# Twelve of the second layer's sixteen output chunks by seven products of combinations, in four sweeps of four chunks

## The chip, the cores and the metric

One Trainium2 chip, one core of it. The metric is the device time of one execution in microseconds (us), a median over runs. Engines are named as in the profile: PE is TensorE (PEld its weight loads), DVE is VectorE, ACT is ScalarE, POOL is GpSimd, SP issues the DMAs.

## The reference, cut to what matters

```python
x = attention(q, k, v)            # 2304 tokens x 512, sliding window
h = x @ moe_w_in                  # 512 -> 2048
x = elu(h) @ moe_w_out            # 2048 -> 512
h = x @ moe2_w_in                 # second layer, same shapes
g = h * (1.0 / (1.0 + np.exp(-h)))
return g @ moe2_w_out             # 2304 x 512
```

Here it is about the last line: g (2304 tokens x 2048) times moe2_w_out (2048 x 512).

## The kernel before, in words

The tokens are three blocks of 768 (`BIG`), each cut into two halves of 384 (`HALF`); the hidden width of 2048 is sixteen chunks of 128. Both layers run in sweeps over chunks: `SWEEPS` (line 174) gives the second layer the chunks 0 to 6, 6 to 12 and 12 to 16. A **step** is one sweep of one block; `steps` (lines 195, 196) lists them, six of the first layer (a first sweep of four chunks was done beside the attention) and nine of the second, in the order of `ORDER` (line 182). The block that ends one sweep begins the next.

Every operand is split into a high and a low fp32r part (`split_weight`, lines 328 to 335, for weights: ACT copies the high part, DVE subtracts). A product is three matmuls: high by high, high by low, low by high.

In a step the hidden values of two chunks at a time (a **quad**, lines 1031 to 1102) are made by seven products of combinations in place of eight: six matmuls of 384 columns each (line 1051). The seven input combinations are the tiles `c`, made on DVE and ACT for a block's first sweep (`make`, lines 920 to 951; for the second layer's first step ahead of time, `make_far`), stored, and loaded again for each later sweep of another block (`reload`, lines 985 to 988, 7 x 768 KB): each is loaded as soon as the last quad of the step before has read that tile. Of the seven accumulated results, ACT copies out three (`snap`, line 1060) and DVE adds to three (line 1064); `activated` (lines 1005 to 1029) then writes, for each of a quad's four results (two chunks x two halves), SiLU by ACT twice (lines 1014, 1015: plain, and rounded to the high part) and the low part by one DVE subtraction (line 1029).

Then `outputs` (lines 1104 to 1163) multiplies by w_out. In the second layer a group is one tile of 128 tokens: for each chunk of the sweep three matmuls of 512 columns (line 1143), all into one PSUM bank; afterwards the bank is copied to (first sweep, ACT, line 1155) or added to (DVE, line 1157) the block's accumulator `acc`. In the last sweep each finished tile is stored (line 1161). The first half's three groups follow the quads; the second half's three are owed to the next step and are merged into its first nine products (`merge`, `SPAN`, lines 1169 to 1205).

Weights come through four raw buffers (`weight`, lines 337 to 394): 64-bit input, turned into fp32 by one POOL, one ACT and two DVE operations (lines 358 to 363) for each of the 32 chunks of a layer, then split. Chunks of w_in go in pairs into three buffers of combinations (`form`, line 387), chunks of w_out into a ring of seven (`OUTS`).

All this is not issued in program order: `Plan` (lines 35 to 133) is a list scheduler that the kernel runs while it is built. Each operation has an engine, a cost in us, the keys it reads and writes, and a due time; per engine the ready operation that is latest is issued next. The chip then runs each engine's list in that fixed order.

Of the kernel before, what the change touches and what calls it, by code (L numbers as in the profile page):

```python
# [22 lines left out]
def f32(ap):  # L23
    return ap.bitcast(F32)
# [112 lines left out]
def attention_elu_silu_kernel(  # L137
# [33 lines left out]
        for g in range(g0, g0 + n):  # L171
            home[g] = bi, (g - g0) * P

    SWEEPS = [(0, 4), (4, 10), (10, 16)], [(0, 6), (6, 12), (12, 16)]
    FIRST_F = SWEEPS[0][0][1]
    MOST_F = 6
    NRAW = 4
# [1 line left out]
    BIG = 6 * P  # L179
    HALF = BIG // 2  # L180
    NBIG = NT // BIG
    ORDER = ((0, 1, 2), (2, 1, 0)), ((2, 1, 0), (0, 1, 2), (2, 1, 0))
    PAIRS, OUTS, BANKS = 3, 7, 3
    GS = 6, 7
    SPAN = 9
# [7 lines left out]
    BURST = 99  # L193

    steps = [(0, sw + 1, b) for sw in range(2) for b in ORDER[0][sw]]
    steps += [(1, sw, b) for sw in range(3) for b in ORDER[1][sw]]
    FAR = 6

    plan = Plan()
# [4 lines left out]
    def matmuls(n, w):  # L204
        return n * (w + 32) / 2400.0
# [85 lines left out]
    bank_n = [0]  # L291
    banks = [BANKS]

    def bank():
        i = bank_n[0] % banks[0]
        bank_n[0] += 1
        return ("m", i)
# [7 lines left out]
                for f in range(f0, f1):  # L305
                    tasks.append((kind, layer, f))
    raw_of, weights = {}, {}
    ring_n = {"raw": 0, "pair": 0, "out": 0}

    def ring(name, n):  # L310
        ring_n[name] += 1
        return (ring_n[name] - 1) % n
# [15 lines left out]
    def split_weight(tag, keys, src, half, w, r, low_eng="DVE"):  # L328

        hi, lo = [tag[:1] + tag[1:] + (j,) for j in range(2)]  # L330
        cost = 0.08 + w / 1040.0
        add("ACT", cost, lambda: nc.scalar.activation(T[hi], f32(src()), AF.Copy), r=r, w=[hi])
        eng = {"DVE": nc.vector, "POOL": nc.gpsimd}[low_eng]
        add(low_eng, cost if low_eng == "DVE" else 1.1,
            lambda: eng.tensor_tensor(T[lo], f32(src()), f32(T[hi]), op=ALU.subtract), r=list(r) + [hi], w=[lo])

    def weight(i):

        t = tasks[i]
        kind, layer, f = t  # L340
        w = ws[layer][kind]
        raw_of[t] = ("scratch",) + SCRATCH[i] if i in SCRATCH else ("raw", ring("raw", NRAW))
        top_k, low_k = raw_keys(t, "top"), raw_keys(t, "low")
        top = lambda: raw_tile(t)[:, :, 1]
        low = lambda: raw_tile(t)[:, :, 0]

        if i < len(HELD):
            hold(lambda: f32(raw_tile(t))[:, 0, 0:1], top_k + low_k, HELD[i])

# [13 lines left out]
        add("DVE", 0.61, lambda: nc.vector.scalar_tensor_tensor(top(), top(), 3, low(), op0=ALU.logical_shift_left,  # L363
                                                               op1=ALU.bitwise_or), r=low_k, w=top_k)
        if layer == 0 and f < FIRST_F:
            tag = ("w0", kind, f)
            split_weight(tag, None, top, None, 4 * P, top_k)
            weights[t] = tag
        elif kind == 1:
            tag = ("w1", ring("out", OUTS))  # L370
            split_weight(tag, None, top, None, 4 * P, top_k)
            weights[t] = tag
        elif f % 2 == 0:
            i = ring("pair", PAIRS)
# [307 lines left out]
    def hidden(bi, f, due):  # L682
# [16 lines left out]
                                 start=(c == 0 and x == 0), stop=(c == NKC - 1 and x == 2))  # L699
        for c in range(NKC):  # L700
            r = raw_keys(t0, "top") + [("xt", bi % 2, c, 0)] if plain else [wt + (0,), wt + (1,), ("x0", 0, c), ("x0", 1, c)]
            tensor(matmuls(4 if plain else 3, w), lambda c=c: piece(c), r=r, w=[m], due=due and due())
        i = e0_n[0] % ES0 if bi < NB - 1 else 0
        e0_n[0] += 1
        ek = ("ex" if i else "e0", i)
# [14 lines left out]
    def output_first(bi, c, due):  # L720
# [33 lines left out]

        def emit(f):
            r = raw_keys((1, 0, f), "top") + plain_keys(f) if plain else [("w0", 1, f, 0), ("w0", 1, f, 1), ("g0", f, 0), ("g0", f, 1)]
            tensor(matmuls(4 if plain else 3, w), lambda: piece(f), r=r, w=[m], due=due and due())
            if f == FIRST_F - 1:
                add("ACT", 0.06 + w / 1200.0 + 0.1 * (w == 4 * P and g0 * P // BIG != (g0 * P + w - 1) // BIG), keep, r=[m], w=ak)
        return emit  # L760
# [128 lines left out]
    def opened_late():  # L889
        early.close()  # L890
        pool = ctx.enter_context(tc.tile_pool(name="late", bufs=1, side="right"))
        for half in range(2):
            for i in range(GS[half]):
                for j in range(2):
                    fixed(pool, ("g", half, i, j), [P, HALF], F32R)
        for i in range(OUTS):
            for j in range(2):
                fixed(pool, ("w1", i, j), [P, 4 * P], F32R)


    def again(k):
# [93 lines left out]
            return "load"  # L995
        return "make" if not any(s[::2] == (layer, b) for s in steps[:k]) else "load"

    ns = {"hs": 0, "h2": 0, "e": 0, "g0": 0, "g1": 0, "below": 0}
    g_of, g_now = {}, {}

    def slot(name, n):
        ns[name] += 1
        return (ns[name] - 1) % n

    def activated(k, f, half, src, sk):

        layer = steps[k][0]
        gi = slot(f"g{half}", GS[half])
        g_of[k, f, half] = gi
        g_now[half, gi] = k, f  # L1010
        gk = [("g", half, gi, j) for j in range(2)]
        ek = ("e", slot("e", ES))
        if layer == 1:
# [90 lines left out]
    def outputs(k):  # L1104
# [6 lines left out]
        for j in range(size):  # L1111
            half = j // (size // 2)
            parts = 2 if k == len(steps) - 1 and j == size - 1 else 1
            for part in range(parts):
# [5 lines left out]
                def piece(fp, st=st, w=w, s=s, jj=jj, half=half):  # L1120
# [4 lines left out]
                    for f in (2 * fp, 2 * fp + 1):  # L1125
                        gi = g_of[k, f, half]
                        assert g_now[half, gi] == (k, f)
                        wt = weights[1, layer, f0 + f]
                        r += [("g", half, gi, x) for x in range(2)] + [wt + (x,) for x in range(2)]
                        items.append((f, gi, wt))  # L1130
# [31 lines left out]
                groups.append((half, [lambda fp=fp, piece=piece: piece(fp) for fp in range(n // 2)]))  # L1162
        return [[g for h, g in groups if h == half] for half in range(2)]

    def open_first(groups):
        n = len(groups[0])
        return [g[i] for i in range(n - 1) for g in groups] + [g[n - 1] for g in groups]
# [11 lines left out]
    def layers():  # L1179
# [15 lines left out]
        for k, (layer, sw, b) in enumerate(steps):  # L1195
            f0, f1 = SWEEPS[layer][sw]
            nq = (f1 - f0) // 2
            weights_to((0, layer, f1 - 1))
            over = []
            order = []  # L1200
# [6 lines left out]
            if k == FAR - 2:  # L1207
                make_far(FAR)
            weights_to((1, layer, f1 - 1))
            first, second_half = outputs(k)  # L1210
            first = open_first(first)
            second_half = [p for g in second_half for p in g]
            first = first[:2] + over[:1] + first[2:3] + over[1:] + first[3:]
            if k + 1 < len(steps) and SPAN:
                owed = second_half
            else:
# [43 lines left out]
```

## Time and profile before

| | |
|---|---|
| median of 3 runs | 865.89 us (865.34 to 866.75) |
| the profiled execution | 865.82 us; its span 864.0 us, so 1.8 us lie around the span |
| granted PE clock | 0.999 of full speed |
| PE, PEld busy | 99%, 90% of the span |
| DVE, ACT, POOL busy | 70%, 58%, 15% |
| DMA | 142.02 MB, mean 164 GB/s |

Busy times are unions over the span. A matmul's duration in a row is its passage through the pipeline; what a matmul costs in a stream is the distance between the starts of two streams, divided by the count.

### The profile page before, as it was taken

The page shows a single profiled execution, that of the slowest core. Times are in us where ns is not written, and L with a number is a line of the kernel's source. Part 1 is how long each engine was busy: PE and PEld are TensorE (multiplying, and loading weights), DVE is VectorE, ACT ScalarE, POOL GpSimd, SP SyncE. Part 2 cuts the span into 40 slices and gives each one's busy share as a digit, 9 for nine tenths or more (in the row PEclk, how much of TensorE's full clock was granted, in tenths as well). Part 3 has the DMA queues.
Part 4 walks back from the last instruction along what each step waited for, and adds up shares of the span by engine and source line. Part 5 has one row for each costly group of instructions (what it writes and reads, how often), then busy time and mean ns, then how long its engine had stood idle before and what let it go on. Part 6 is the DMA issues. An engine that isn't in the chain of part 4 may idle for free.

```text
span 864.0 us, 15329 instructions
## 1 busy us (share of the span) xinstructions
PE 855.2 (99%) x5654; PEld 778.3 (90%) x5654; DVE 602.8 (70%) x1402; ACT 501.7 (58%) x1203; POOL 127.6 (15%) x227
## 2 busy tenths in 40 slices
PE   8999999999999999999999999999999999999998
PEld 5788877779999999999999998989898989989997
DVE  8989998966998688896779687636665335633333
ACT  7888977865856474644567484747572325433331
POOL 6264544411010001100001110001110000100000
PEclk9999999999999999999999999999999999999999
DMA  9666775668720222551848254152255050226721
GB/s 303 241 209 190 244 244 187 213 214 329 294 108 1 62 68 80 178 200 52 330 155 329 74 202 176 74 206 74 74 167 211 27 229 29 69 82 224 265 88 73
DMA packets 67962, 142.02 MB, mean 164 GB/s; under 512 B 4400, under 2 KB 50224, under 8 KB 67888
## 3 DMA queue, kind: packets, MB, share of 16 engines
q1 hardware_dynamic: 67312, 140.53, 45.9%
q8 instruction: 44, 0.72, 0.3%
q10 hardware_dynamic: 576, 0.52, 0.2%
q14 instruction: 30, 0.25, 0.1%
HBM read 104.07 MB, written 36.96 MB: 163 GB/s over the span
## 4 chain that ended last, share of the span: by engine, by line
PE 92%; DMA 4%; ACT 2%; DVE 1%; POOL 1%; issue 0%; SPq 0%; POOLq 0%; ACTq 0%; DVEq 0%
PE m L1143 40%; PE m L1051 36%; PE m L737 5%; PE m L698 5%; PE a L619 2%; PE s L526 2%; PE t L586 2%; DMA raw<-in_moe_w_in_dram 1%; ACT p L545 1%; DMA q<-in_q_dram 1%; DMA d<-st 1%; DMA acc<-xd 1%; DMA xd<-xt 1%; ACT pt L595 0%; PE m L731 0%
## 5 line engine op out<-in xcount | busy, mean ns | idle before, releaser
L1143 PE MATMUL m<-w,g 128*128 128x512 f32 (+1 forms) x876 | 211.9, 387 | 0.0
L1143 PEld LDWEIGHTS m<-w,g 128*128 128x128 f32 x876 | 161.6, 188 | 26.2
L1143 PE MATMUL m<-g,w 128*128 128x384 f32 x864 | 161.6, 336 | 0.0
L1143 PEld LDWEIGHTS m<-g,w 128*128 128x128 f32 x864 | 151.8, 188 | 0.0
L1029 DVE TENSOR_TENSOR g<-e,g 128x384 fp32r<-128x384 f32 x168 | 94.0, 568 | 50.3 <-ACT e L1014 43.6
L358 POOL TENSOR_SCALAR raw<-raw 128x512 f32<-128x512 f32 x60 | 46.6, 777 | 543.3 <-DMA raw<-in_moe_w_out_dram 223.7
L1064 DVE TENSOR_TENSOR hs<-m,hs 128x384 f32<-128x384 f32 x84 | 46.7, 556 | 90.4 <-PE m L1051 88.2
L1051 PE MATMUL m<-c,wd 128*128 128x384 f32 x504 | 101.3, 335 | 0.0
L1051 PE MATMUL m<-c,wc 128*128 128x384 f32 x504 | 101.2, 335 | 0.0
L1051 PE MATMUL m<-c,wa 128*128 128x384 f32 x504 | 98.9, 336 | 0.0
L1051 PEld LDWEIGHTS m<-c,wa 128*128 128x128 f32 x504 | 89.2, 188 | 2.6
L1051 PEld LDWEIGHTS m<-c,wc 128*128 128x128 f32 x504 | 89.2, 188 | 2.0
L1051 PEld LDWEIGHTS m<-c,wd 128*128 128x128 f32 x504 | 89.1, 188 | 2.0
L1060 ACT ACTIVATE hs<-m 128x384 f32<-128x384 f32 x84 | 41.2, 490 | 83.1 <-PE m L1051 82.8
L1157 DVE TENSOR_TENSOR acc<-m,acc 128x384 f32<-128x384 f32 (+2 forms) x85 | 51.5, 606 | 52.8 <-PE m L1143 52.2
L567 POOL TENSOR_SCALAR p<-p,sums 128x192 f32<-128x192 f32 x112 | 65.0, 597 | 69.6 <-DVE sums L559 41.8
L545 ACT ACTIVATE p<-p,neg 128x192 f32<-128x192 f32 (+1 forms) x144 | 63.0, 443 | 3.9 <-DVE neg L537 3.9
L1015 ACT ACTIVATE g<-hs 128x384 fp32r<-128x384 f32 x48 | 25.3, 526 | 54.7 <-DVE hs L1064 54.6
L1051 PE MATMUL m<-c,wb 128*128 128x384 f32 x252 | 50.7, 335 | 0.0
L737 PE MATMUL m<-g,w 128*128 128x512 f32 (+1 forms) x240 | 47.8, 351 | 0.5 <-DVE ex L714 0.5
L698 PE MATMUL m<-x,w 128*128 128x512 f32 (+1 forms) x240 | 48.2, 353 | 0.0
L361 DVE SCALAR_TENSOR_TENSOR raw<-raw 128x512 uint32<-128x512 uint32 x60 | 43.7, 730 | 4.6 <-POOL raw L358 3.3
(149 smaller groups left out, 1212.9 us busy)
## 6 DMA issues: line engine op xcount, KB each, us to landing
c<-d SPq DMA_DIRECT2D x63, 768.0 KB, 6.7
raw<-in_moe_w_in_dram SPq DMA_DIRECT2D x32, 512.0 KB, 5.9
raw<-in_moe_w_out_dram SPq DMA_DIRECT2D x28, 512.0 KB, 3.6
d<-c SPq DMA_DIRECT2D x14, 768.0 KB, 4.2
d<-st SPq DMA_DIRECT2D x19, 384.0 KB, 3.4
k<-in_k_dram SPq DMA_DIRECT2D x16, 384.0 KB, 5.0
d<-xs SPq DMA_DIRECT2D x14, 384.0 KB, 2.8
v<-in_v_dram SPq DMA_DIRECT2D x18, 256.0 KB, 4.0
```

Of the source, the lines that this page charges most:

```text
L358: add("POOL", 0.66, lambda: nc.gpsimd.tensor_scalar(f32(top()), f32(top()), 2.0 ** -112, 1.0, op0=ALU.mult, op1=ALU.mult), w=top_k)
L361: add("DVE", 0.61, lambda: nc.vector.scalar_tensor_tensor(low(), top(), 0x80000000, low(), op0=ALU.bitwise_and, op1=ALU.bitwise_or), r=top ...
L545: nc.scalar.activation(dst, dst, AF.Exp, bias=T["neg", u % 4][:, i:i + 1], scale=-1.0, accum_out=T["sm", u % MS][:, e, j:j + 1])
L567: nc.gpsimd.tensor_scalar(dst, dst, T["sm", u % MS][:, e, j:j + 1], 1.0, op0=ALU.mult, op1=ALU.mult)
L698: nc.tensor.matmul(T[m][:, 0:w], a[:, cs], T["x0", b2][:, c, 0:w], start=(c == 0 and x == 0), stop=(c == NKC - 1 and x == 2))
L737: nc.tensor.matmul(T[m][:, 0:w], a[:, cs], b2[:, 0:w], start=(f == 0 and x == 0), stop=(f == FIRST_F - 1 and x == 2))
L1029: add("DVE", 0.475, lambda: nc.vector.tensor_tensor(T[gk[1]], T[ek], f32(T[gk[0]]), op=ALU.subtract), r=[ek, gk[0]], w=[gk[1]])
L1051: nc.tensor.matmul(T[m][:, 0:HALF], a[:, cs], x[:, j, c, :], start=(begin and c == 0 and n == 0), stop=(c == 1 and n == 2), skip_group_che ...
L1060: add("ACT", 0.4, lambda: nc.scalar.activation(T[s], T[m][:, 0:HALF], AF.Copy), r=[m], w=[s])
L1064: add("DVE", 0.475, lambda: nc.vector.tensor_tensor(T[s], T[m][:, 0:HALF], T[s], op=ALU.add), r=[m], w=[s], port=False)
L1143: nc.tensor.matmul(T[m][:, 0:w], l, rr, start=(f == 0 and x == 0), stop=(f == n - 1 and x == 2))
L1157: add("DVE", 0.08 + w / 960.0, lambda: nc.vector.tensor_tensor(dst, T[m][:, 0:w], dst, op=ALU.add), r=[m], w=dk, port=False)
```

## The change

The second layer gets four sweeps of four chunks. The first stays as it was. In the other three (chunks 4 to 16), two chunks and the block's two halves on one side, and the two chunks and the two halves of 256 output columns on the other, form 2x2 blocks, and w_out is applied by seven products of combinations in place of eight. `y_weight` makes a pair's four combinations (`form`) and splits them; `seven_activated` makes the seven combinations of a quad's four activations (four `form` on DVE) and `place` splits each into one of the thirteen `g` places; `seven_outputs` runs each product for two token tiles, then for the third, as matmuls of 256 columns, and adds each result to `acc` from a bank that the next product of its chain goes on filling. Five products follow the quads, two (7 and 4) are owed to the next step. The cost of 0.435 us that replaces a formula in two places is a number for the scheduler.

```diff
-    SWEEPS = [(0, 4), (4, 10), (10, 16)], [(0, 6), (6, 12), (12, 16)]
+    SWEEPS = [(0, 4), (4, 10), (10, 16)], [(0, 4), (4, 8), (8, 12), (12, 16)]
...
-    ORDER = ((0, 1, 2), (2, 1, 0)), ((2, 1, 0), (0, 1, 2), (2, 1, 0))
+    ORDER = ((0, 1, 2), (2, 1, 0)), ((2, 1, 0), (0, 1, 2), (2, 1, 0), (0, 1, 2))
...
-    steps += [(1, sw, b) for sw in range(3) for b in ORDER[1][sw]]
+    steps += [(1, sw, b) for sw in range(len(SWEEPS[1])) for b in ORDER[1][sw]]
...
+    kept = set()
+
     def bank():
+        while bank_n[0] % banks[0] in kept:
+            bank_n[0] += 1
         i = bank_n[0] % banks[0]
         bank_n[0] += 1
         return ("m", i)
...
+    def seven(layer, f):
+        return layer == 1 and f >= SWEEPS[1][0][1]
...
+        kind, layer, f = t
+        w2 = 2 * P
...
+        if f % 2 == 0:
+            i = weights[t] = ring("ypair", 2)
+            if ring_n["ypair"] <= 2:
...
+            b11 = part(t, 0, 1)
+            split_weight(("yb", i), None, b11[0], None, w2, b11[1])
+            return
+        t0 = (kind, layer, f - 1)
+        i = weights[t] = weights[t0]
+        (b11, b12), (b21, b22) = ([part(tt, x, 1) for x in range(2)] for tt in (t0, t))
+        (t1, t2), (t3, t4) = ([part(tt, x, 0) for x in range(2)] for tt in (t0, t))
+
+        def form(d, x, y):
+            add("DVE", 0.34, lambda: nc.vector.tensor_tensor(d[0](), x[0](), y[0](), op=ALU.subtract), r=x[1] + y[1], w=d[1])
+        src, r = whole(t, 1)
+        split_weight(("w1", 3 * i), None, src, None, 4 * P, r)
+        form(t1, b12, b11)
+        form(t2, b22, t1)
+        src, r = whole(t0, 0)
+        split_weight(("w1", 3 * i + 1), None, src, None, 4 * P, r)
+        form(t3, b22, b12)
+        form(t4, b21, t2)
+        src, r = whole(t, 0)
+        split_weight(("w1", 3 * i + 2), None, src, None, 4 * P, r)
...
+        elif kind == 1 and seven(layer, f):
+            y_weight(t)
         elif kind == 1:
-            tag = ("w1", ring("out", OUTS))
+            tag = ("w1", 3 + f if layer else ring("out", OUTS))
             split_weight(tag, None, top, None, 4 * P, top_k)
             weights[t] = tag
...
             r = raw_keys(t0, "top") + [("xt", bi % 2, c, 0)] if plain else [wt + (0,), wt + (1,), ("x0", 0, c), ("x0", 1, c)]
-            tensor(matmuls(4 if plain else 3, w), lambda c=c: piece(c), r=r, w=[m], due=due and due())
+            tensor(0.435 if plain else matmuls(3, w), lambda c=c: piece(c), r=r, w=[m], due=due and due())
...
+        for i in range(2):
+            for j in range(2):
+                T["yb", i, j] = T["w1", OUTS - 1, j][:, i * 2 * P:(i + 1) * 2 * P]
...
+    places, combo, a_of, pending, owed_place = [], {}, {}, [], {}
...
+    def place(k, q, i, src, sk):
+
+        assert places
+        gk = combo[k, q, i] = places.pop(0)
+        assert not g_unread.get(gk, 0), (k, q, i, gk)
+        hi, lo = (("g",) + gk + (j,) for j in range(2))
+        add("ACT", 0.42, lambda: nc.scalar.activation(T[hi], src(), AF.Copy), r=[sk], w=[hi])
+        add("DVE", 0.475, lambda: nc.vector.tensor_tensor(T[lo], src(), f32(T[hi]), op=ALU.subtract), r=[sk, hi], w=[lo])
+
+    def seven_activated(k, f, half, src, sk):
+
+        q = f // 2
...
+        a_of[k, q, half, f % 2] = view, key
+        add("ACT", 0.42, lambda: nc.scalar.activation(view(), src(), AF.Silu), r=[sk], w=[key])
+        if (half, f % 2) != (1, 0):
+            place(k, q, {(0, 0): 1, (0, 1): 2, (1, 1): 4}[half, f % 2], view, key)
+            return
+        a11, a12, a21, a22 = (a_of[k, q, h, x] for h in range(2) for x in range(2))
+
+        def form(d, x, y, op=ALU.subtract):
+            add("DVE", 0.475, lambda: nc.vector.tensor_tensor(d[0](), x[0](), y[0](), op=op), r=[x[1], y[1]], w=[d[1]])
+        form(a22, a21, a22, ALU.add)
+        place(k, q, 5, *a22)
+        form(a21, a11, a21)
+        form(a11, a22, a11)
+        place(k, q, 6, *a11)
+        form(a12, a12, a11)
+        place(k, q, 3, *a12)
+        if q:
+            pending.append(lambda: place(k, q, 7, *a21))
+        else:
+            place(k, q, 7, *a21)
...
+        if is_seven(k):
+            seven_activated(k, f, half, src, sk)
+            return
...
+    SEVEN = {1: ("yb", 0), 2: (0, 0), 3: (0, 2 * P), 4: (2, 2 * P), 5: (1, 0), 6: (1, 2 * P), 7: (2, 0)}
+    CHAIN = (1, "b", 0, 0), (2, "a", 0, 0), (5, "c", 1, 1), (6, "b", 0, 1), (3, "c", 0, 1), (7, "b", 1, 1), (4, "b", 1, 0)
...
+        def group(i, chain, rows, cols, tiles):
+            tag, o = SEVEN[i]
+            begin = (chain, tiles) not in held
+            if begin:
+                held[chain, tiles] = bank()
+            m = held[chain, tiles]
+            if i in (2, 3, 4):
+                kept.discard(m[1])
+            else:
+                kept.add(m[1])
+            r = []
...
+            for q in range(nq):
+                gk = combo[k, q, i]
+                pi = weights[1, layer, f0 + 2 * q]
+                wk = ("yb", pi) if tag == "yb" else ("w1", 3 * pi + tag)
+                r.append((gk, wk))
...
+            def products():
+                for q, (gk, wk) in enumerate(r):
+                    gh, gl = (T[("g",) + gk + (j,)] for j in range(2))
+                    h, lo = (T[wk + (j,)] for j in range(2))
+                    for x, (a, b2) in enumerate(((gh, h), (gh, lo), (gl, h))):
+                        for n, jj in enumerate(tiles):
+                            nc.tensor.matmul(T[m][:, n * w:(n + 1) * w], a[:, jj * P:(jj + 1) * P], b2[:, o:o + w],
+                                             start=(begin and q == 0 and x == 0 and n == 0),
+                                             stop=(q == nq - 1 and x == 2 and n == len(tiles) - 1), skip_group_check=True)
+            tensor(matmuls(3 * nq * len(tiles), w), products,
+                   r=[("g",) + gk + (j,) for gk, _ in r for j in range(2)] + [wk + (j,) for _, wk in r for j in range(2)], w=[m])
+            row = rows * 3 + tiles[0]
+            dst = lambda: acc[b].rearrange("p (r d) -> p r d", d=DM)[:, row:row + len(tiles), cols * w:(cols + 1) * w]
+            dk = [x for n in range(len(tiles)) for x in acc_keys(b, (row + n) * DM + cols * w, (row + n) * DM + (cols + 1) * w)]
+            size = len(tiles) * w
+            add("DVE", 0.08 + size / 960.0, lambda: nc.vector.tensor_tensor(
+                dst(), T[m][:, 0:size].rearrange("p (n d) -> p n d", d=w), dst(), op=ALU.add), r=[m], w=dk, port=False)
+            if last and (i, cols) in ((2, 0), (3, 1), (7, 1), (4, 0)):
+                r0 = b * BIG + row * P
+                load(lambda: nc.sync.dma_start(out[r0:r0 + len(tiles) * P, cols * w:(cols + 1) * w].rearrange("(n p) d -> p n d", p=P),
+                                               dst()), size * P * 4, r=dk, due=clock[0] + 3.0)
+
...
+        for i, chain, rows, cols in CHAIN:
+            for n, tiles in enumerate(((0, 1), (2,))):
+                def fn(i=i, chain=chain, rows=rows, cols=cols, tiles=tiles, n=n):
+                    group(i, chain, rows, cols, tiles)
+                    if n == 1:
+                        freed(i)
+                        while pending and places:
+                            pending.pop(0)()
+                parts.append(fn)
+        return parts[:2 * 5], parts[2 * 5:]
...
+            if is_seven(k) and not places:
+                used = [x for x in g_unread if g_unread[x]]
+                places.extend(x for x in [(h, i) for h in range(2) for i in range(GS[h])] if x not in used)
+                places.extend(used)
...
-            first, second_half = outputs(k)
-            first = open_first(first)
-            second_half = [p for g in second_half for p in g]
-            first = first[:2] + over[:1] + first[2:3] + over[1:] + first[3:]
+            if is_seven(k):
+                for fn in over:
+                    fn()
+                first, second_half = seven_outputs(k)
+            else:
```

## Rows read from the trace of the kernel before

**Rows 1.** The page: busy us, share of the span, instructions of each engine

```profile
PE 855.2 (99%) x5654; PEld 778.3 (90%) x5654; DVE 602.8 (70%) x1402; ACT 501.7 (58%) x1203; POOL 127.6 (15%) x227
```

**Rows 2.** Waits of PE, whole span, longest: us in total, times, longest us

```profile
PE m L731 <- ACT acc L745: 1.9, 1, 1.9
```

**Rows 3.** Windows: length, then busy us (instructions) of PE, PEld, DVE, ACT, POOL; PEclk, DMA share, GB/s

```profile
216.00:237.60 21.60, 21.60 (x126) 21.60 (x125) 21.23 (x41) 17.32 (x34) 2.01 (x3) 1.00 0.78 293
237.60:259.20 21.60, 21.60 (x125) 21.60 (x124) 19.67 (x38) 11.16 (x23) 2.61 (x3) 1.00 0.30 109
...
453.60:475.20 21.60, 21.60 (x126) 21.60 (x126) 20.29 (x40) 15.97 (x32) 2.37 (x3) 1.00 0.85 329
...
790.50:821.50 31.00, 31.00 (x158) 28.11 (x158) 11.69 (x20) 10.20 (x22) 0.00 (x0) 1.00 0.66 227
```

**Rows 4.** Lines by form: count, busy us, mean ns of one

```profile
L1143 PE MATMUL m<-w,g 128*128 128x512 f32 x852 | 209.0, 390 | 0.0
...
L1143 PE MATMUL m<-w,g 128*128 128x256 f32 x24 | 3.0, 283 | 0.0
...
L1143 PEld LDWEIGHTS m<-w,g 128*128 128x128 f32 x876 | 161.6, 188 | 26.2
```

**Rows 5.** Timeline of PE: start us, us, what

```profile
80.41 3.14 PE L698 MATMUL m<-x,w 128*128 128x256 f32 x24
...
514.63 8.33 PE L1143 MATMUL m<-w,g 128*128 128x512 f32 x36
522.80 1.21 PE L1051 MATMUL m<-c,wa 128*128 128x384 f32 x6
...
545.56 1.20 PE L1051 MATMUL m<-c,wc 128*128 128x384 f32 x6
546.60 1.20 PE L1051 MATMUL m<-c,wd 128*128 128x384 f32 x6
...
857.75 3.03 PE L1143 MATMUL m<-w,g 128*128 128x256 f32 x24
```

**Rows 6.** Timeline of DVE in two dense stretches

```profile
219.60 0.69 DVE L363 SCALAR_TENSOR_TENSOR raw<-raw 128x512 uint32<-128x512 uint32 x1
220.20 0.55 DVE L1029 TENSOR_TENSOR g<-e,g 128x384 fp32r<-128x384 f32 x1
220.67 0.68 DVE L335 TENSOR_TENSOR w<-raw,w 128x512 fp32r<-128x512 f32 x1
...
519.57 2.17 DVE L905 TENSOR_TENSOR c<-acc,c 128x384 fp32r<-128x384 f32 x4
...
527.36 0.41 DVE L387 TENSOR_TENSOR raw<-raw,raw 128x256 f32<-128x256 f32 x1
527.69 0.42 DVE L387 TENSOR_TENSOR raw<-raw 128x256 f32<-128x256 f32 x1
```

**Rows 7.** Lines by form of DVE, the span: count, busy us, mean ns

```profile
L1157 DVE TENSOR_TENSOR acc<-m,acc 128x512 f32<-128x512 f32 x35 | 24.2, 692 | 44.6 <-PE m L1143 44.6
...
L1157 DVE TENSOR_TENSOR acc<-m,acc 128x256 f32<-128x256 f32 x2 | 0.8, 424 | 1.8 <-PE m L1143 1.8
```

**Rows 8.** Timeline, a POOL conversion and the DVE operations beside it

```profile
228.24 0.68 POOL L358 TENSOR_SCALAR raw<-raw 128x512 f32<-128x512 f32 x1 [13.64 <-DMA raw<-in_moe_w_out_dram]
...
228.29 0.55 DVE L1064 TENSOR_TENSOR hs<-m,hs 128x384 f32<-128x384 f32 x1
228.96 0.69 DVE L361 SCALAR_TENSOR_TENSOR raw<-raw 128x512 uint32<-128x512 uint32 x1
```

**Rows 9.** Timeline, from one quad result to its low part

```profile
823.67 0.56 DVE L1064 TENSOR_TENSOR hs<-m,hs 128x384 f32<-128x384 f32 x1 [1.46 <-PE m L1051]
...
824.70 0.51 ACT L1014 ACTIVATE e<-hs 128x384 f32<-128x384 f32 x1
...
825.24 0.56 DVE L1029 TENSOR_TENSOR g<-e,g 128x384 fp32r<-128x384 f32 x1 [1.01 <-ACT e L1014]
```

**Rows 10.** The page, DMA issues: count, KB each, median us to landing

```profile
c<-d SPq DMA_DIRECT2D x63, 768.0 KB, 6.7
```

More of the change, by code (lines that the diff above doesn't have):

```diff
@@ L307, in attention_elu_silu_kernel @@
     raw_of, weights = {}, {}
-    ring_n = {"raw": 0, "pair": 0, "out": 0}
+    ring_n = {"raw": 0, "pair": 0, "out": 0, "ypair": 0}
     def ring(name, n):
@@ L335, in split_weight, with y_weight @@
             lambda: eng.tensor_tensor(T[lo], f32(src()), f32(T[hi]), op=ALU.subtract), r=list(r) + [hi], w=[lo])
+    def seven(layer, f):
+        return layer == 1 and f >= SWEEPS[1][0][1]
+    def y_weight(t):
+        kind, layer, f = t
+        w2 = 2 * P
+        part = lambda tt, x, word: (lambda: f32(raw_tile(tt)[:, x * w2:(x + 1) * w2, word]), [raw_keys(tt, "top" if word else "low")[x]])
+        whole = lambda tt, word: (lambda: raw_tile(tt)[:, :, word], raw_keys(tt, "top" if word else "low"))
+        if f % 2 == 0:
+            i = weights[t] = ring("ypair", 2)
+            if ring_n["ypair"] <= 2:
+                add(None, 0.0, None, w=[x for j in range(2) for x in (("yb", i, j), ("w1", OUTS - 1, j))])
+            b11 = part(t, 0, 1)
[17 more added lines that the diff above has]
+        split_weight(("w1", 3 * i + 2), None, src, None, 4 * P, r)
     def weight(i):
@@ L756, in emit @@
             r = raw_keys((1, 0, f), "top") + plain_keys(f) if plain else [("w0", 1, f, 0), ("w0", 1, f, 1), ("g0", f, 0), ("g0", f, 1)]
-            tensor(matmuls(4 if plain else 3, w), lambda: piece(f), r=r, w=[m], due=due and due())
+            tensor(0.435 if plain else matmuls(3, w), lambda: piece(f), r=r, w=[m], due=due and due())
             if f == FIRST_F - 1:
@@ L996, in source @@
         return "make" if not any(s[::2] == (layer, b) for s in steps[:k]) else "load"
-    ns = {"hs": 0, "h2": 0, "e": 0, "g0": 0, "g1": 0, "below": 0}
-    g_of, g_now = {}, {}
+    ns = {"hs": 0, "h2": 0, "e": 0, "g0": 0, "g1": 0, "below": 0, "a": 0}
+    g_of, g_now, g_unread = {}, {}, {}
     def slot(name, n):
@@ L1003, in slot, with is_seven @@
         return (ns[name] - 1) % n
+    def is_seven(k):
+        return seven(steps[k][0], SWEEPS[steps[k][0]][steps[k][1]][0])
+    places, combo, a_of, pending, owed_place = [], {}, {}, [], {}
+    A_TILES = [("e", i) for i in range(ES)] + [("xs", i, j) for i in range(2) for j in range(2)] + [("t2",), ("t3",)]
+    def place(k, q, i, src, sk):
[7 more added lines that the diff above has]
+        q = f // 2
+        key = A_TILES[slot("a", len(A_TILES))]
+        if key[0] == "xs":
+            view = lambda: T["xs",][:, key[1], key[2] * HALF:(key[2] + 1) * HALF]
+        else:
+            view = lambda: T[key]
+        a_of[k, q, half, f % 2] = view, key
[17 more added lines that the diff above has]
+            place(k, q, 7, *a21)
     def activated(k, f, half, src, sk):
         layer = steps[k][0]
+        if is_seven(k):
+            seven_activated(k, f, half, src, sk)
+            return
         gi = slot(f"g{half}", GS[half])
@@ L1010, in activated @@
         g_now[half, gi] = k, f
+        g_unread[half, gi] = 2 * NKC // 2 if layer == 0 else BIG // P // 2
         gk = [("g", half, gi, j) for j in range(2)]
@@ L1127, in piece @@
                         assert g_now[half, gi] == (k, f)
+                        g_unread[half, gi] -= 1
                         wt = weights[1, layer, f0 + f]
@@ L1163, in outputs, with seven_outputs, freed @@
         return [[g for h, g in groups if h == half] for half in range(2)]
+    SEVEN = {1: ("yb", 0), 2: (0, 0), 3: (0, 2 * P), 4: (2, 2 * P), 5: (1, 0), 6: (1, 2 * P), 7: (2, 0)}
+    CHAIN = (1, "b", 0, 0), (2, "a", 0, 0), (5, "c", 1, 1), (6, "b", 0, 1), (3, "c", 0, 1), (7, "b", 1, 1), (4, "b", 1, 0)
+    def seven_outputs(k):
+        layer, sw, b = steps[k]
+        f0, f1 = SWEEPS[layer][sw]
+        nq = (f1 - f0) // 2
+        w = DM // 2
+        last = sw == len(SWEEPS[1]) - 1
+        held, begun = {}, set()
+        def group(i, chain, rows, cols, tiles):
[35 more added lines that the diff above has]
+                                               dst()), size * P * 4, r=dk, due=clock[0] + 3.0)
+        def freed(i):
+            for q in range(nq):
+                places.append(combo[k, q, i])
+        parts = []
+        for i, chain, rows, cols in CHAIN:
[8 more added lines that the diff above has]
+        return parts[:2 * 5], parts[2 * 5:]
@@ L1209, in layers @@
             weights_to((1, layer, f1 - 1))
-            first, second_half = outputs(k)
-            first = open_first(first)
-            second_half = [p for g in second_half for p in g]
-            first = first[:2] + over[:1] + first[2:3] + over[1:] + first[3:]
+            if is_seven(k):
+                for fn in over:
+                    fn()
+                first, second_half = seven_outputs(k)
+            else:
+                first, second_half = outputs(k)
+                first = open_first(first)
+                second_half = [p for g in second_half for p in g]
+                first = first[:2] + over[:1] + first[2:3] + over[1:] + first[3:]
             if k + 1 < len(steps) and SPAN:
```

## The prediction, as it was made before the result

> **What bounds the kernel now.** The page's first part comes first: PE is busy 99% of the span, DVE 70%, ACT 58% [rows 1]. A busy PE can still be a waiting one, so the list of PE's waits is next: its longest single wait is 1.9 us, in the attention stage, and no line of the two layers is in that list [rows 2]. The windows say the same of the layers' stages: PE 21.60 of 21.60 us at a granted clock of 1.00, also where DVE is busy 98% of the time [rows 3]. So the second layer is a stream of matmuls without gaps. Whatever shortens the stream shortens the run, until another engine can't feed it.
>
> What a matmul costs in that stream is read from starts in PE's timeline [rows 5]: 36 of 512 columns from 514.63 to 522.80, 0.2269 us each; six of 384 columns from 545.56 to 546.60, 0.1733 us. For 256 columns there is one stretch in the same code, the last tile of the run, cut into halves: 24 in 3.03 us, of which the last one's own passage is 0.283 us [rows 4], so 23 distances of 0.1194 us. Every one has a weight load of its own.
>
> **The matmuls.** Removed: twelve chunks x 18 token tiles x 3 = 648 of 512 columns, 12 of them run as 24 halves today: 636 x 0.2269 + 24 x 0.1194 = 147.2 us. Added: nine steps x 2 quads x 7 products x 3 tiles x 3 = 1134 of 256 columns, at 0.1194 us 135.4 us. That is a gain of 11.8 us, not the eighth of 18 us, as a matmul costs some 13 ns beside its columns and there are 474 more. The other 24-long stretch of that shape, in the attention stage, took 3.14 us [rows 5], 0.1242 us each; by it the gain is 6.4 us. I take the first, from the same operands, and keep the second for the range. The w_in products stay 24 quads, whatever the sweeps.
>
> A weight load lasts 188 ns on average [rows 4], longer than 0.1194 us; but in that stretch of 24 each had its load and they came 0.1194 us apart, so the loads overlap one another and the matmuls. The Trainium skill ("TensorE: Matmul & The Clock Gate", Part 3, The mechanism) says that a load overlaps matmuls in flight only if their row groups differ, and Part 2 (LDWEIGHTS) puts 128 columns at 107 ns. By an estimate from that, the 474 extra loads would add 51 us; the stretch of 24 speaks against it.
>
> **VectorE.** This is the price. In streams, starts of DVE operations lie 0.47 us apart for 384 columns, 0.60 for 512, 0.33 for 256 [rows 6], although one lasts 0.55, 0.69 and 0.42 us [rows 6, 7]. Per new step: each quad has 3 sums (line 1064), 4 new forms and 7 low parts (4 before), so 28 x 0.47 = 13.2 us; each of 7 products is added to acc in two pieces of 512 and 256 columns, 7 x 0.93 = 6.5 us. Together 19.7 us, where a step of four chunks has 11.7 us busy now [rows 3]. Per sweep come the weights of the next: 16 conversions x 0.60, twelve low parts x 0.60 and four x 0.33, 16 forms x 0.33 (half of these are new): 23.4 us. Each of 8 POOL conversions can push a DVE operation back: beside one the next start came after 0.67 us in place of 0.47 [rows 8], so 1.6 us. A sweep needs 3 x 19.7 + 23.4 + 1.6 = 84.1 us of DVE, against 3 x (84 x 0.1733 + 126 x 0.1194) = 88.8 us of PE: 94.7%. This holds for the first and the second new sweep; the last has no weights to make for a next one and stays near 70%.
>
> The densest long stretch that the trace shows without a wait of PE is 216.0 to 259.2: DVE 40.9 of 43.2 us, 94.7% as well [rows 3]. So there is no reserve. Between 94.7% filled (nothing lost) and 88% (95.6 us a sweep, 13.6 us lost in two) I take 93%, nearer to those rows: 90.4 us a sweep, **3.3 us lost** in two. The work has freedom, since weights may be made at any point of a sweep, but a chain in `seven_activated` has less of it: an operation on what the one before wrote starts later.
>
> The Trainium skill ("VectorE: DVE Perf Modes", The DRAIN you can't avoid) says that the next DVE operation does not start until the pipe of the one before is empty. The rows disagree, 0.47 against 0.55 us; what the rule would cost is the fourth rival.
>
> **The chain at the end of the quads.** A product of `seven_outputs` starts only when the combinations of both quads are there. The last quad's last result has to become a22, then combination 5. By the chain of today [rows 9], sum start to low part start is 1.57 us with one SiLU waited for and a second one behind it; with a sum (0.6), SiLU (0.5), form (0.6), copy (0.5), low part (0.6) and some 0.07 us at each hand-over I get 3.1 us. Products 1 and 2 run before it, 36 x 0.1194 = 4.3 us. Slack 1.2 us, with three visits to a DVE that is nearly full: behind half an operation each they cost 0.8 us, behind two operations each 3.2. So 0 to 2.0 us a step; I take 0.25, nearer to the half operations: **2.3 us** in nine steps. Product 2 needs a SiLU, a copy and a low part behind a matmul that runs before or beside product 1's 2.15 us, so it is less late. The adds are in front of products 6, 3, 7 and 4, which go on in the same banks; between an add's product and the next one in its bank lie at least 0.7 us, and only in the final step, where nothing lies between, I count 0.2 us.
>
> **Edits that cost nothing, and their cover.** ACT: 11 operations a quad in place of 8 and five more splits a sweep, about 19 us of a 29.6 us step; it delays only what hangs on it above. Reloads: two more steps of seven 768 KB loads (11 MB), also two more times through SP's queue in front of the stores. A tile is read again one step's end later, seven products and 10.8 us of outputs: 18 us, and a load lands 6.7 us after its issue [rows 10]; seven in a row at the 329 GB/s of a busy stretch [rows 3] take 17 us and are wanted one by one over 13 us more. Steps of four chunks with a reload run today with PE full [rows 3]. Without that cover it is 1 to 3 us in each of six steps. The stores become 24 in place of 19, behind the same adds; the last one stays 128 KB. The first sweep has four chunks, so `make` for its second step has 2.7 us less behind outputs (12 x 0.2269): its last DVE operations ended 1.1 us before PE's next step [rows 5, 6]; I take 0.5 us, 0 to 2.7. The scheduler's new number for the early products may reorder the attention stage: 0, between -1 and 1.
>
> **The sum.** Against the profiled execution's 865.8 us (the median is 865.9): -11.8 + 3.3 + 2.3 + 0.2 + 0.5 = **860.3 us**.
>
> **The rivals.**
> 1. All is hidden: VectorE's freedom suffices, as at 216 us. 865.8 - 11.8 + 0.2 = 854.2 us. For it: PE never waited at 98% over 21.6 us; against it: that was not 178 us long.
> 2. VectorE becomes the bound, in the first two new sweeps. It decides where DVE can't be kept filled above 84.1 / 93.2 = 90.2%, which eats the 8.8 us left by the other terms. At 88% it is 865.8 - 11.8 + 13.6 + 3.0 = 870.6 us, slower than before. For it: chains of forms, DVE and ACT taking turns; against it: the three dense windows.
> 3. The 256-column matmul does not keep its pace in long runs, so the change doesn't save what it says: bound by loads of 188 ns, 1134 x 0.188 = 213.2 us in place of 135.4, 938 us in all. Only the 24-long stretches speak of it, and against it.
> 4. DVE operations hold the engine for their whole duration (0.55, 0.69, 0.42 us): 28 x 0.55 + 7 x 1.11 = 23.2 us a step and 27.6 us for weights, 98.8 us a sweep, 20 us lost in two, 877 us. Starts in the trace exclude it where operations don't depend on each other.
>
> **How the numbers follow.** A measurement of this kernel can tell 0.2%, 1.7 us, from no change. My forecast with its neighbourhood from 856 to 864.2 us has 0.41; all hidden 0.27; a stop between 864.2 and 867.6 us, VectorE at about 90%, 0.11; VectorE the bound with more than that 0.18; loads or whole durations 0.03. So faster 0.68, same 0.11, slower 0.21. The range goes from 853.5 (all hidden, less what 0.01 us in a start makes over 1134 matmuls) to 872.0 us (88% and a chain that comes late), which leaves out 2 in 10; its upper end also takes in the matmul at 0.1242 us.
>
> **What would show it.** Right: 6128 matmuls; those of 256 columns some 0.12 us apart; DVE busy near 700 us and above 90% in the first two new sweeps; PE waiting in its list of waits for low parts and splits on DVE, some 6 us in all, the more in those two sweeps. DMA near 153 MB. Wrong: a stretch of 256-column matmuls without waits well above 0.12 us each; PE's waits in the layers of more than 12 us or below 1 us; waits on `c` loads, on the raw weights' loads or on ACT ahead of those on DVE.

## The result, and the profile after

The changed kernel takes 852.12 us (median of 4 runs, 851.77 to 852.53) against 865.75 us, a ratio of 0.9841 with a 95% interval of 0.9824 to 0.9858: 13.6 us faster. The forecast was 860.3 us, its range 853.5 to 872.0. The sign was right, the gain was more than twice the forecast, and the time lies 1.4 us below the range, next to the first rival (854.2 us). The profiled execution took 851.86 us, its span is 850.1 us.

The page's first part, which answers to [rows 1]:

```profile
PE 841.6 (99%) x6128; PEld 790.7 (93%) x6128; DVE 711.1 (84%) x1653; ACT 539.3 (63%) x1269; POOL 123.8 (15%) x227
```

Matmuls are 6128 as counted. DVE got 108 us more to do. The list of PE's waits, which answers to [rows 2], with the longest and the only one of the two layers:

```profile
PE m L485 <- DVE warm L473: 1.3, 1, 1.3
...
PE m L1142 <- ACT e L1105: 0.2, 1, 0.2
```

The windows of the three new sweeps (length, then busy us of PE, PEld, DVE, ACT, POOL), which answer to [rows 3]. Each runs from product 1 of a sweep's first step to product 1 of the next sweep's; the third stops 4.1 us ahead of the span's end:

```profile
593.95:682.82 88.87, 88.87 (x632) 88.87 (x632) 84.76 (x172) 53.56 (x108) 6.75 (x8) 1.00 0.45 165
682.82:771.70 88.88, 88.88 (x632) 88.88 (x632) 86.10 (x174) 52.66 (x107) 6.33 (x7) 1.00 0.46 168
771.70:846.00 74.30, 74.23 (x544) 74.03 (x544) 56.07 (x115) 32.15 (x68) 0.00 (x0) 1.00 0.47 171
```

A sweep lasts 88.9 us (88.8 were forecast) and DVE is busy 84.8 and 86.1 us of the first two (84.1 were counted): 95.4% and 96.9%, and PE does not wait once in either. PE's timeline from the last product of the first new step's quads into its outputs, which answers to [rows 5]:

```profile
592.89 1.21 PE L1142 MATMUL m<-c,wb 128*128 128x384 f32 x6
593.95 2.31 PE L1292 MATMUL m<-w,g 128*128 128x256 f32 x18
596.10 1.21 PE L1142 MATMUL m<-c,wa 128*128 128x384 f32 x6
597.14 8.78 PE L1292 MATMUL m<-w,g 128*128 128x256 f32 x72
605.76 1.21 PE L1142 MATMUL m<-c,wa 128*128 128x384 f32 x6
```

Product 1 is the 18, products 2, 5, 6 and 3 the 72: (605.76 - 597.14) / 72 = 0.1197 us each, in a stream three times as long as that of [rows 5] (0.1194). In between, at 596.10, runs the first product of the next step.

**Where the time went.** The first matmul on the combinations `c` divides the run into the attention stage with the first sweep, whose code did not change, and the rest:

```profile
205.49 2.24 PE L1051 MATMUL m<-c,wa 128*128 128x384 f32 x12
```

before, and in the changed kernel

```profile
202.73 2.24 PE L1142 MATMUL m<-c,wa 128*128 128x384 f32 x12
```

So of the 13.9 us between the spans 2.8 came before that point, and 658.5 - 647.4 = 11.1 us behind it. The two are taken apart below.

### The profile page after: what moved, and what is told of

Same layout as the page of the kernel before. It is cut to its first block, busy times and chain, and to the rows that moved or that the text cites. A ratio compares the mean times of both kernels' runs of the same rounds, so it can differ in the third digit from the quotient of the medians.

```text
span 850.1 us, 16650 instructions
## 1 busy us (share of the span) xinstructions
PE 841.6 (99%) x6128; PEld 790.7 (93%) x6128; DVE 711.1 (84%) x1653; ACT 539.3 (63%) x1269; POOL 123.8 (15%) x227
## 2 busy tenths in 40 slices
DMA packets 72241, 153.12 MB, mean 180 GB/s; under 512 B 4704, under 2 KB 54880, under 8 KB 72160
## 4 chain that ended last, share of the span: by engine, by line
PE 94%; DMA 2%; DVE 2%; ACT 1%; POOL 1%; issue 0%; POOLq 0%; DVEq 0%; ACTq 0%
PE m L1142 36%; PE m L1235 23%; PE m L1292 16%; PE m L738 5%; PE m L777 5%; PE a L659 3%; PE s L566 2%; PE t L626 2%; DMA raw<-in_moe_w_in_dram 2%; ACT p L585 0%; PE m L771 0%; DVE acc L399 0%; ACT w L336 0%; DVE t L979 0%; ACT raw L398 0%
## 5 line engine op out<-in xcount | busy, mean ns | idle before, releaser
L1292 PE MATMUL m<-w,g 128*128 128x256 f32 x1134 | 143.5, 282 | 0.1
L1292 PEld LDWEIGHTS m<-w,g 128*128 128x128 f32 x1134 | 141.5, 190 | 0.3 <-DVE acc L1301 0.3
L1142 PE MATMUL m<-c,wa 128*128 128x384 f32 x504 | 98.8, 336 | 0.2 <-ACT e L1105 0.2
L607 POOL TENSOR_SCALAR p<-p,sums 128x192 f32<-128x192 f32 x112 | 61.6, 567 | 72.3 <-DVE sums L599 31.1
L1301 DVE TENSOR_TENSOR acc<-m,acc 128x512 f32<-128x512 f32 (+1 forms) x126 | 66.2, 549 | 4.9 <-PE m L1292 3.9
L1120 DVE TENSOR_TENSOR g<-e,g 128x384 fp32r<-128x384 f32 x96 | 53.4, 570 | 10.5 <-ACT e L1105 5.1
L1235 PE MATMUL m<-w,g 128*128 128x512 f32 x216 | 53.6, 390 | 0.0
L1235 PEld LDWEIGHTS m<-w,g 128*128 128x128 f32 x216 | 40.2, 188 | 6.4
```

The source lines that it names most:

```text
L607: nc.gpsimd.tensor_scalar(dst, dst, T["sm", u % MS][:, e, j:j + 1], 1.0, op0=ALU.mult, op1=ALU.mult)
L1120: add("DVE", 0.475, lambda: nc.vector.tensor_tensor(T[gk[1]], T[ek], f32(T[gk[0]]), op=ALU.subtract), r=[ek, gk[0]], w=[gk[1]])
L1142: nc.tensor.matmul(T[m][:, 0:HALF], a[:, cs], x[:, j, c, :], start=(begin and c == 0 and n == 0), stop=(c == 1 and n == 2), skip_group_che ...
L1235: nc.tensor.matmul(T[m][:, 0:w], l, rr, start=(f == 0 and x == 0), stop=(f == n - 1 and x == 2))
L1292: nc.tensor.matmul(T[m][:, n * w:(n + 1) * w], a[:, jj * P:(jj + 1) * P], b2[:, o:o + w], start=(begin and q == 0 and x == 0 and n == 0), ...
L1301: add("DVE", 0.08 + size / 960.0, lambda: nc.vector.tensor_tensor(dst(), T[m][:, 0:size].rearrange("p (n d) -> p n d", d=w), dst(), op=ALU ...
```

## The experiments

"c to end" is the span less that start, in each run's profile; the medians are whole runs.

| kernel | median us | kernel before beside it | start of c | c to end |
|---|---|---|---|---|
| before | 865.89 | | 205.49 | 658.5 |
| changed | 852.12 | 865.75 | 202.73 | 647.4 |
| after_again | 852.95 | 865.84 | 204.16 | 647.6 |
| after_5 | 852.74 | 865.82 | 203.54 | 647.7 |
| a_formula | 853.66 | 866.10 | 205.72 | 647.7 |
| a_formula_5 | 854.96 | 865.82 | 205.78 | 647.4 |
| b_cost | 863.44 | 866.10 | 205.39 | 658.5 |
| c_sweeps | 863.73 | 866.10 | 203.62 | 658.6 |
| g_cost45 | 852.61 | 865.82 | 203.84 | 647.6 |
| d_low1 | 853.60 | 865.84 | 205.89 | 647.9 |
| d_low2 | 857.85 | 866.10 | 204.99 | 652.2 |
| d_low4 | 872.25 | 865.82 | 203.49 | 668.0 |
| f_gate | 853.90 | 865.84 | 202.75 | 648.8 |
| e_chain | 853.22 | 865.84 | 203.09 | 648.1 |

Behind c the three profiles of the changed kernel agree within 0.3 us. Ahead of it they spread over 1.4 us, and over 3.2 us with d_low1, whose lists are the same there.

### The 2.8 us ahead of the second layer

```diff
# a_formula, a_formula_5: the changed kernel with
-            tensor(0.435 if plain else matmuls(3, w), ...)
+            tensor(matmuls(4 if plain else 3, w), ...)
# b_cost: the kernel before with the opposite edit; both in hidden and output_first
```

> The changed kernel with the scheduler's old cost formula (0.48 us) for the 32 early products of the first block, in place of 0.435. Theory 1, the two gains are separate and the early 2.8 us come from this number: 854.6 to 855.0 us, the first product on the combinations c starts near 205.5 us again, and the second layer lasts as long as in the changed kernel. Theory 2, the early gain comes from the second layer's due times, handed back through the scheduler: 852.1 us, as the changed kernel, within 0.7.

> The kernel before with 0.435 us as the cost of those 32 products, and nothing else. Theory 1: 863.0 us (865.8 less 2.8), the first product on c near 202.7 us. Theory 2: 865.8 us within 0.9, no change.

b_cost: 863.44 against 866.10 us beside it, ratio 0.9973 (0.9963 to 0.9983), so 2.7 us for a number in the scheduler, as by theory 1. Its profile does not show them: the profiled execution, 865.72 us, was the slowest of ten, and c began at 205.39 us in it and not near 202.7. a_formula came out between the theories (853.66 us, runs from 852.51 to 855.13, the changed kernel not on the same chip), so the pair was measured once more, side by side:

> The changed kernel, unaltered, with more rounds, beside the next one on one chip. 852 to 853.5 us. From the first product on c to the end of the span 647.4 us, as in its first profile, whatever the attention stage takes.

> The changed kernel with the old cost formula for the early products, with more rounds. The lists of the engines up to the second layer are then those of the kernel before. If the number is worth what the kernel before showed with it (863.4 against 866.1): 2.7 us more than the changed kernel beside it. If most of the early gain of the first pair of profiles was the spread of the attention stage from run to run: 0 to 1 us more.

854.96 against 852.74 us: 2.2 us, and behind c no difference. Theory 2 falls with that, and for another reason too: in the traces the operations of PE up to 498 us, those of DVE and ACT up to 458 us and all of POOL's come in the same order in a_formula and the kernel before, and in b_cost and the changed kernel. By these pairs the number is worth 2.2 to 2.7 us; all runs of the changed kernel with the old number (median of 9: 854.37 us) and with the new one (median of 12: 852.52 us), over several chips, give 1.9. It makes the scheduler think that an early product of the first block ends sooner (0.435 for 0.48 us), and that changes the order of the attention stage, in the traces from the 269th matmul on, at 22.9 us. Which of the operations that moved saves the time is not shown. A third value:

> The changed kernel with 0.45 us in place of 0.435 for the early products, which is what two matmul instructions of 0.225 us each take in the attention stage. If a cost nearer to the measured one gives a better list: 0 to 1 us less than the changed kernel. If one list is as good as another by luck: anything within 2.5 us of it, the second layer unchanged at 647.4 to 647.7 us from the first product on c.

852.61 us, the same as after_5 (852.74). So it is not that 0.435 is the one right number; 0.45 does as well.

### Sweeps without the seven products

```diff
     def seven(layer, f):
-        return layer == 1 and f >= SWEEPS[1][0][1]
+        return False
...
-            tag = ("w1", 3 + f if layer else ring("out", OUTS))
+            tag = ("w1", ring("out", OUTS))
```

> Four sweeps of four chunks in the second layer and the 0.435, but w_out as before (512 columns, eight products), so without the seven products. Matmul counts are those of before. If sweeps and reloads cost nothing beside PE, as predicted: 863.0 us with theory 1 (865.8 with theory 2). Rival, that two more steps of reloads, an added pass over acc and the shorter cover of make cost 1 to 3 us each: 866 to 869 us.

863.73 us, as b_cost; behind c 658.6 us, as the kernel before (658.5). Two more steps of reloads, the added pass over acc and the shorter cover of `make` cost nothing beside PE. The whole 11.1 us is due to the seven products.

### How much more VectorE can take

```diff
 # in place(); S = (7,), (7, 1), (7, 1, 2, 4)
+        for _ in range(1 + (i in S)):
-        add("DVE", 0.475, ...T[lo], src(), f32(T[hi])...)
+            add("DVE", 0.475, ...T[lo], src(), f32(T[hi])...)
```

> The changed kernel with the low part of combination 7 alone computed twice: 2 more VectorE operations in each new step, 2.8 us a sweep, so 86.9 us of need against 88.8 us of PE, 98%. If VectorE is felt only where its need passes PE's time: no change in the second layer, 0 to 0.7 us. If a filling of some 96.5% (what the changed kernel has) is all that it gives: 90.1 us a sweep, 1.2 us lost in each of two sweeps and 2.5 to 3 us in all.

> The changed kernel with the low parts of combinations 7 and 1 computed twice: 4 more VectorE operations of 0.47 us in each of the nine new steps, 17 us in all, 5.6 us a sweep. By the count of the prediction VectorE then needs 89.7 us of a sweep in which PE needs 88.8. If VectorE is felt only where its need passes PE's time: 852 to 854 us. If it is felt from about 95% on, as the prediction's 93% filling had it: 96.5 us a sweep in two sweeps, 15 us lost, 860 us or more.

> The changed kernel with four of the seven low parts (7, 1, 2, 4) computed twice: 8 more VectorE operations a step, 11.3 us a sweep, 95.4 us of need against 88.8 us of PE in the first two new sweeps. If VectorE is the bound above 100%: 13 to 16 us in all, VectorE busy above 97% in those two sweeps and steps of some 31.8 us there, while the last sweep, at about 75 of 88.8 us, keeps 29.6 us a step. If the 4.7 us that two doubled low parts cost were waits in their chains and not the bound: some 9 us, in the last sweep as well.

| | need of a sweep, counted | of PE's 88.8 us | c to end, more than 647.6 |
|---|---|---|---|
| changed | 84.1 us | 95% | 0 |
| d_low1 | 86.9 us | 98% | 0.3 us |
| d_low2 | 89.7 us | 101% | 4.6 us |
| d_low4 | 95.4 us | 107% | 20.4 us |

At 98% there is next to nothing; from 101% on it costs. So VectorE is felt somewhere between 98 and 101% of PE's time, not at 93%, and the changed kernel, at 95%, stands in front of that edge. The place is as in the first forecast of each run; the size is not. d_low2, at 857.85 us, lies between its two forecasts: its need is above PE's time by 0.9 us in each of two sweeps, and it lost 0.3, 2.8 and 1.8 us in the three, so in the last one too, where DVE's need is below PE's time. Around each of its four longest waits of PE DVE was full, here in its second new sweep,

```profile
695.00:700.00 5.00, 4.42 (x33) 4.10 (x31) 5.00 (x13) 1.91 (x4) 0.00 (x0) 1.00 0.54 171
```

and 4.93 of 5.00 us from 769 to 774, 3.90 of 4.00 from 784 to 788, 6.00 of 6.00 from 792 to 798. The first two windows of d_low4, in which a sweep began 0.8 us later to begin with:

```profile
594.71:685.10 90.39, 89.50 (x630) 88.46 (x630) 88.84 (x178) 49.92 (x102) 6.05 (x7) 1.00 0.45 160
685.10:780.60 95.50, 91.62 (x631) 90.44 (x630) 92.32 (x191) 50.81 (x104) 4.90 (x7) 0.98 0.43 153
```

DVE is at 98.3 and 96.7% of them. But the count (13 to 16 us) fell short, and the last sweep did not keep its pace as I had expected of it: the sweeps grew by 1.5, 6.6 and 12.5 us (the last, to the end of the span, took 90.9 us for 78.4). What was late is seen in d_low4's waits of PE:

```profile
PE m L1293 <- ACT w L336: 5.7, 1, 5.7
PE m L1293 <- DVE acc L1302: 3.5, 5, 1.7
...
PE m L1293 <- DVE g L1062: 0.6, 1, 0.6
```

The last line speaks on the rival of d_low4's forecast, waits in the chains of the doubled low parts: only 0.6 us of d_low4's 13.0 us of waits behind c are for a low part, and only 0.6 of d_low2's 3.0 (one wait each). The others are for PSUM banks that DVE or ACT had not yet read, and for weights. With DVE full around them, this speaks for DVE's load and against the doubled operations' own chains.

The longest wait is for a weight of w_out, in the first step of the last sweep, where PE waited 5.7 us at a stretch. As far as these waits show, what comes late when DVE is too full is the next sweep's weights, and that sweep's first step pays. The wait had a price of its own. PE stood still from 790.25 to 795.96 us; the windows from 792 us on, with the granted clock ahead of the DMA share:

```profile
792.00:796.00 4.00, 0.04 (x1) 0.04 (x1) 3.93 (x8) 2.60 (x6) 0.00 (x0) 0.73 0.00 0
796.00:800.00 4.00, 3.97 (x17) 3.67 (x18) 4.00 (x10) 1.47 (x3) 0.00 (x0) 0.50 0.00 0
800.00:804.00 4.00, 4.00 (x33) 4.00 (x33) 3.47 (x9) 0.68 (x1) 0.00 (x0) 0.91 0.31 102
```

The clock fell to 0.50 (1.2 of 2.4 GHz) while PE was idle and came back while it ran: 17 matmuls in those 4 us, 33 in the next. It did not take so long a wait: in the sweep before, behind waits of 0.4, 1.7 and 0.6 us between 697.7 and 704.5 us, the clock was at 0.50 as well,

```profile
706.00:708.00 2.00, 2.00 (x8) 2.00 (x8) 2.00 (x5) 0.64 (x1) 1.20 (x2) 0.50 1.03 335
```

and six matmuls of 384 columns from 705.96 to 707.88 came 0.320 us apart, for 0.173 elsewhere.

### The chain behind a step's last quad

```diff
# f_gate: product 3 of a step writes the scheduler's key ("gate",), every product on c reads it
-   r=[...wk...], w=[m])
+   r=[...wk...], w=[m] + [("gate",)] * (i == 3))
-   r=[(tag, pi, 0), (tag, pi, 1)] + c_keys(i), w=[m])
+   r=[(tag, pi, 0), (tag, pi, 1)] + c_keys(i) + [("gate",)], w=[m])
# e_chain, in place():
+        for _ in range(5 if q and i == 5 else 1):
             add("ACT", 0.42, ...T[hi], src(), AF.Copy...)
```

> The changed kernel again, unaltered, beside the next three, since the attention stage of one and the same program was seen to end up to 2.5 us apart from run to run. 851.8 to 853.5 us; the second layer, from the end of the first layer's last products to the end of the span, as long as in its first profile within 0.3 us.

> The changed kernel with one more order in the scheduler: the next step's first products wait until product 3 of this step is issued, so no product of the next step runs between products 1 and 2. Cover in front of product 5 falls from 6.4 to 5.3 us behind the quad's last result. By the rows of the changed kernel (low part 5 ready some 4.3 us behind it): nothing, 0 to 0.5 us. By the prediction's price of this chain, made for this very order: 0.25 us a step, 2.3 us.

> The changed kernel with the ACT copy of the second quad's combination 5 done five times: the chain behind the quad's last result grows by 4 x 0.43 = 1.7 us, ACT by 1.7 us a step, VectorE by nothing. If 6.4 us of cover stand against 4.3 us of chain: 0 to 1 us in all. By the prediction's slack of 1.2 us: 0.5 us and its 0.25 us a step, 6 to 7 us.

f_gate costs 1.2 us behind c (648.8 against 647.6). Of that 1.1 us fall in the first new step, where 72 + 18 matmuls from 593.90 on end 1.1 us late. There PE came behind DVE three times: the matmuls at 597.49 and 603.99 waited for a low part, the one at 603.28 for an add to acc, and DVE was busy 11.84 of these 11.87 us (in the changed kernel 11.78 of 11.81 us, without a wait). The seven steps behind it take 29.68 us on average in place of 29.62. So with 1.1 us less cover the chain that I had priced at 0.25 us a step costs some 0.05, beside that first step; the 4.3 us of cover that I had in mind were in no run. e_chain, 1.7 us longer, costs 0.5 us in all, as by the rows of the changed kernel, not 6 to 7; its cover was again 6.4 us in the second new step, but 7.4 in the first, where the scheduler put one more product in. The rows are DVE's and ACT's timeline in the changed kernel's second new step, and answer to [rows 9]:

```profile
623.67 0.55 DVE L1155 TENSOR_TENSOR h<-m,h 128x384 f32<-128x384 f32 x1
...
624.80 0.56 DVE L1079 TENSOR_TENSOR xs<-xs 128x384 f32<-128x384 f32 x1
...
625.87 1.02 DVE L1061 TENSOR_TENSOR g<-xs,g 128x384 fp32r<-128x384 f32 x2
```

```profile
624.25 0.53 ACT L1072 ACTIVATE xs<-h 128x384 f32<-128x384 f32 x1
...
625.18 0.94 ACT L1060 ACTIVATE g<-xs 128x384 fp32r<-128x384 f32 x2
```

PE ended the quad's product 3 at 622.53 and began its product 4. The sum began 1.1 us later, behind other work of DVE, then SiLU, form a22, copy, low part: ready at 626.9 at the latest, 4.4 us behind PE (3.1 us without waits and some 0.8 for DVE were forecast, so the delays were a little larger than taken). But product 5 of the outputs started at 626.76 + 18 x 0.1197 = 628.9, 6.4 us behind.

## Why the prediction was wrong

**What held.** The price of the matmuls: 0.1197 us for 0.1194, on which the 11.8 us rest; c to end gave 11.1. Weight loads don't bind: 72 matmuls with a load each came 0.1197 us apart. The Trainium skill's rule ("TensorE: Matmul & The Clock Gate", Part 3, The mechanism), that loads overlap matmuls only across row groups, would have shown as much more, and did not; the same section also lets a load go ahead into a background weight buffer, which these rows leave open. VectorE's work per sweep: 84.1 us counted, 84.8 and 86.1 busy. That its operations start 0.47 us apart and not a duration apart held as well: 98.8 us would not have fitted into 88.9. That is against the first sentences of the Trainium skill's "VectorE: DVE Perf Modes", The DRAIN you can't avoid, which the prediction took as the whole rule; the section goes on that an operation that is not held starts earlier, and with that the trace agrees. DMA 153.12 MB (153); reloads and stores hidden (c_sweeps). Loads that set the pace and whole durations were rivals 3 and 4, and both are out.

**The step that failed first: the losses, 6.3 us.** All of them together were 0.7 us (11.8 forecast without them, 11.1 measured), and PE's waits in the layers came out below 1 us, which the prediction had named as a sign that it is wrong. By terms:

- VectorE, 3.3 us, in fact 0: I took 93% as what DVE can be filled to, though the rows showed 94.7% over 43 us and 98% over 21.6 us without a wait of PE. Those were stretches where that much work was there, not a ceiling. The runs put the edge between 98 and 101% of counted need (d_low1, d_low2). A reason that fits, not tested by itself, is that the next sweep's weights, 23.4 of the 84.1 us counted, may lie anywhere in a sweep.
- The chain, 2.3 us, in fact 0: its length was about right, its cover was not. I laid PE's order out as the program lists it. The scheduler places ready work into it: the quad's product 4 went behind product 3 and the next step's first product between products 1 and 2, so 6.4 us lie ahead of product 5 and not 4.3. f_gate shows that 5.3 us nearly suffice; 4.3 were not tried.
- `make`, 0.5 us, and the final step, 0.2 us: these two held, and they are the whole 0.7. At the end of the first sweep's first step, at 504.90, two matmuls come 0.4 us late in all; it is the one wait in the list, for a SiLU on ACT, which by the trace made combinations `c` between its SiLUs there. In the final step 0.3 us are lost to an add on DVE, as foreseen; the row is the weight load's:

```profile
844.12 2.21 PEld L1292 LDWEIGHTS m<-w,g 128*128 128x128 f32 x18 [0.27 <-DVE acc L1301]
```

**The second: "the scheduler's new number, 0, between -1 and 1".** It was -1.9 to -2.7 us (all runs, a_formula_5, b_cost). I had treated it as noise around nothing. The attention stage is not a stream without gaps as the layers are (in the kernel before PE is busy 2.14 of the 4.00 us from 40 to 44); there an order had 2 us and more in it. This term alone put the result outside the range: 865.8 - 11.1 = 854.7 us lies inside it, and with 1.9 to 2.7 us less it is 852.8 to 852.0. The range's lower end, 853.5, had not even the -1 in it that the term itself was given. That the number helped and did not hurt is luck: nothing in the prediction spoke for a sign.

**The second rival** was right in its mechanism and its place (d_low2, d_low4: VectorE above PE's time, weights late at the start of the next sweep), wrong in where it sets in: not at 90.2% filling but between 98 and 101% of counted need, which this change does not reach.

## What to carry to other kernels

Where a bound engine runs without gaps, price the change in its own instructions at the shape that it will have, and compare a second engine's work with the first one's time over the whole stretch in which the work may move: up to 98% it cost 0.3 us or nothing here, above 100% more than the excess (4.6 us for 1.8, 20.4 for 13.2). Before a latency chain is charged, ask what the scheduler can place in front of it. And an edit to a scheduler's cost is an edit to the order of everything near it: measure it alone.

## What the runs showed of the hardware that was not expected

VectorE ran at 96.9% for 89 us beside a PE that never waited; in the densest slice of it, in the changed kernel,

```profile
742.80:764.40 21.60, 21.60 (x163) 21.60 (x162) 21.50 (x45) 11.25 (x24) 0.75 (x1) 1.00 0.09 29
```

at 99.5%. In d_low4 TensorE's granted clock fell to half twice, behind one wait of 5.7 us and behind three of 0.4 to 1.7 us; after the first, 16 matmuls of 256 columns came 0.213 us apart in place of 0.120, so a late weight cost some 1.5 us more than its lateness. And the attention stage of identical lists ended anywhere from 202.73 to 205.89 us, while in the three profiles of the changed kernel everything behind it repeated within 0.3 us.
